# Linear attention into a two-layer MLP: the first microseconds of a kernel listed anew

## Chip, cores and metric

The kernel runs on one core of one Trainium2 chip. The metric is device time in microseconds, the median of several runs. Beside the runs there is one profiled execution, of which the trace tells every instruction; its span is a little shorter than its time. TensorE is PE, VectorE DVE, ScalarE ACT, GpSimd POOL and SyncE SP in what follows.

## The reference

Two parts follow on each other. The first is a linear attention with a decaying state, for 4 batches, 8 heads, 768 tokens and 48 values a head:

```python
for t in range(S):
    cur = np.einsum('bhd,bhe->bhde', u[None] * kt, vt)
    y[:, :, t] = np.einsum('bhd,bhde->bhe', rt, state + cur)
    state = w[None, :, :, None] * state + np.einsum('bhd,bhe->bhde', kt, vt)
```

The second takes y as 3072 rows of 384 through two matrices, with a leaky ReLU between them:

```python
h = x @ w_in                    # 384 to 2048
g = np.maximum(0.01 * h, h)
return (g @ w_out).astype(np.float32)   # 2048 to 384
```

## The kernel before

**Stages.** The tokens are cut in chunks of 128, and one chunk of one batch, with all 8 heads, is a stage: 24 stages n, batch n % 4, chunk n // 4. Inside a chunk the attention is written as matmuls. r and k are first multiplied with tables of powers of w (qtab, ktab, line 344), which are made once: w is spread over 128 partitions by a matmul with a vector of ones (line 295), ACT takes the logarithm (line 301), and an exponential with a scale that depends on the token gives the table (line 306). One state per batch is carried from chunk to chunk, so stage n needs the state that stage n - 4 left.

**Steps of a stage**, by the letters that the list of the work uses:

- k, r, v: the loads of the stage (line 222, by POOL's queue; those of stage 0 by ACT's and SP's, line 213). wi and wo are the quarters of the two matrices (lines 232 and 236), also on POOL's queue.
- P: product of r (q) or k with its table, on DVE (line 344). T: its transpose by a matmul with the identity, on PE (line 398). t: the copy of that out of PSUM, on ACT (line 412) or, with @, on DVE (line 410). From stage 8 on, X with a T is a transposing DMA on SP's queue instead (line 349).
- A: scores of the 8 heads, on PE (line 423). M: their causal mask, on DVE, in two halves (line 432, from stage 8 on line 436).
- X: product of the transposed q and k (line 359, DVE); D: its sum with w and u over each head (line 451, PE); Q: v scaled by that (line 366, DVE). From stage 8 on q (lines 373 to 377, DVE) and Q (line 384, POOL) take their place.
- K: the stage's addition to the state (line 464, PE). S: the new state (lines 522 to 527, DVE).
- Y: the stage's output (lines 550 and 557, PE); y: its copy into xT (line 571, ACT).
- G n.g: a quarter of the first matrix for one stage, 12 matmuls of 128 columns (line 596); g: the leaky ReLU (line 606, ACT). J m.j: an eighth for two stages, 6 matmuls of 256 columns (line 619); j: line 629. H: the second matrix for a stage (line 643, PE); h: the copy and the store on SP's queue (lines 655 and 657).
- F n: n matmuls of ones that nobody reads (line 260), here called fillings.

**Order.** For the first four stages' MLP, and for the attention of the stages ahead of it, everything stands in one list, `ORDER`, written out by hand. Each name adds instructions to its engine, and each engine runs its own in the order of the list. The waits follow from what is read and written (`Sched.add`, `Sched.resolve`): a step behind a waiting one on the same engine waits too. PSUM has eight banks, which `take` and `give` pass around in the order of the list. After the list comes a regular loop over pairs of stages, from stage 6 on for the MLP (lines 696 to 727).

**Single steps** of the list, once each: w, u (rows), w8, u8 (by heads) are small loads; tcol, exps the exponents; ones, one, v0z, qk0, wlz memsets on DVE; id, tri the identity and the triangle on POOL; table the loading of ACT's functions; id8 a small float32 identity and wu8 the product of w and u (DVE); Cm columns of w and w times u by heads (lines 484 and 485, PE), Wl their logarithm, C their copies, W the decay table of the state (lines 497, 504 and 512); u16, U, utab the spread of u (lines 317, 321 and 326).

Before the change w is spread in two halves of 192 columns, each with a matmul, a logarithm and two exponentials of its own: bcA, bcB, lnA, lnB, ktabA, qtabA, ktabB, qtabB.

Of the kernel before, what the change touches and what calls it, by code (L numbers as in the profile page):

```python
# [17 lines left out]
HD = H * D  # L18
# [6 lines left out]
FIRST, NB, PACE = 6, B, 3  # L25
TURNED, DIAG, CARRY, EXACT = 8, 8, 4, 1
ORDER = """
w k0 r0 u8 w8 u ones tcol wi0 v0z r2 table exps one id wlz qk0 F6 bcA r1 id8 F2 bcB lnA k1 u16 wu8 ktabA F1 Cm k2 lnB U
qtabA ktabB v0 utab P0k qtabB Wl wi3 F6 T0k P0q W C tri t0k@ F1 T0q v1 P1q t0q P2q F6 T1q X0 r3 A0 P1k t1q T2q M0a T1k
k3 t2q D0 P2k F1 K0 t1k Q0 T2k v2 M0b t2k F1 A1 X1 v5 F2 Y0 X2 M1b A2 k4 y0 D2 M1a D1 K1 G0.0 k5 Q1 M2b G0.3 g0.0 wi1  # L30
P3q Y1 P3k g0.3 r4 S1 T3q y1 K2 Q2 T3k t3q v3 G1.3 S2 t3k M2a G1.0 r5 g1.3 P4k Y2 X3 g1.0 r8 P5k A3 S0 y2 K5 M3b r6 T5k
G2.3 t5k S5 k7 G2.0 g2.3 M3a G1.1 k9 g2.0 P4q G0.1 g1.1 wi2 T4k g0.1 D3 P5q K3 r7 T4q Q3 t4k T5q G2.1 S3 t5q k6 P8q Y3
t4q P6q X5 A5 v4 g2.1 P7k A4 X4 y3 D5 T6q M4a wo3 T7k t6q G3.0 M5a v8 t7k G3.3 Q5 g3.0 wo0 M5b D4 G3.1 g3.3 P9k k8 G2.2
M4b g3.1 P7q G1.2 wo2 g2.2 P6k T7q v6 g1.2 T6k t7q@ K4 Y5 t6k Q4 wo1 A7 y5 X6 A6 k11 S4 Y4 M7b v9 D6 y4 G3.2 M6a v10
J2.4 M6b g3.2 J2.3 M7a v11 j2.4 J2.5 X7 j2.3 r10 D7 J2.1 j2.5 q8 r9 J2.2 j2.1 J2.6 r11 j2.2 P8k J2.0 j2.6 v7 X8T K8 Q6
K6 j2.0 G0.2 k10 S6 Y6 g0.2 S8 J2.7 y6 H1 j2.7 P11k K9 H2 h1 S9 P10q H0 h2 P9q q9 X9T P11q K7 Q9 H3 Q7 h0 X11T S7 P10k
X10T Q8 Y7 h3 A9 y7 A8 M9a M8a M9b M8b k12 r12 v12 k13 r13 v13
"""


# [4 lines left out]
class Sched:  # L45
# [7 lines left out]

    def add(self, eng, emit, R=(), W=(), dma=None):
        o = Op()
        o.eng, o.emit, o.dma, o.inc, o.val = eng, emit, dma, False, None
        deps = []
        for key in R:
            w = self.writer.get(key)
            if w is not None:  # L60
                deps.append((w, True))
        for key in W:
            w = self.writer.get(key)
            if w is not None:
                deps.append((w, False))
            for r in self.readers.get(key, ()):
                deps.append((r, False))
        o.deps = []
        for d, raw in deps:
            if d.dma is None and d.eng == eng and dma is None and (eng == "pe" or not raw):  # L70
                continue
            if d is not o and d not in o.deps:
                o.deps.append(d)
        for key in R:
            self.readers.setdefault(key, []).append(o)
        for key in W:
            self.writer[key] = o
            self.readers[key] = []
        self.ops.append(o)
        return o  # L80
# [47 lines left out]
def bass_rwkv5_eagle__then__act_leaky_relu_kernel(  # L128
# [19 lines left out]
    r_sb = SB("r_sb", [128, NST, HD])  # L148
    k_sb = SB("k_sb", [128, NST, HD])
    v_sb = SB("v_sb", [128, NST, H * E])  # L150
    w_row = SB("w_row", [1, HD], FP32)
    u_row = SB("u_row", [1, HD], FP32)
    one_row = SB("one_row", [1, 128], FP32)
    u_row16 = SB("u_row16", [1, HD])
    w_head = SB("w_head", [H, D], FP32)
    u_head = SB("u_head", [H, D], FP32)
# [4 lines left out]
    lnw = SB("lnw", [128, HD], FP32)  # L161
# [3 lines left out]
    qtab = SB("qtab", [128, HD])  # L165
    ktab = SB("ktab", [128, HD])
    tcol = SB("tcol", [128, 1], FP32)
    qexp = SB("qexp", [128, 1], FP32)
    kexp = SB("kexp", [128, 1], FP32)
    wcol = SB("wcol", [128, NP], FP32)  # L170
    wl = SB("wl", [128, NP, 2 * D])
    ones = SB("ones", [128, 256])
    mask = SB("mask", [128, 128])
    ident = SB("ident", [128, 128])
    ku = [SB(f"ku{i}", [128, HD]) for i in range(4)]
# [2 lines left out]
    qk = [SB(f"qk{i}", [128, 2 * H, E]) for i in range(NQK)]  # L178
# [5 lines left out]
    xT = [SB(f"xT{i}", [128, NSL, 256]) for i in range(NX)]  # L184
    gT = [SB(f"gT{i}", [128, NFB, 256]) for i in range(NG)]
    out_sb = [SB(f"out_sb{i}", [128, HD], FP32) for i in range(NO)]
    ps = [ctx.enter_context(nc.psum_tensor(f"ps{i}", [128, 512], FP32)) for i in range(8)]

    V, A, PE, SP, G = nc.vector, nc.scalar, nc.tensor, nc.sync, nc.gpsimd
    sch = Sched(ctx, nc)  # L190
    add = sch.add
    free = list(range(8))

    def take():
        i = free.pop(0)
# [19 lines left out]
    def load_one(n, which, pace=()):  # L215
# [39 lines left out]
    def fill(n):  # L255
        i = free[0]

        def emit():
            for _ in range(n):
                last = PE.matmul(ps[i][:, 0:256], ones[:, 0:128], ones[:, 0:256], start=True, stop=True)  # L260
            return last

        add("pe", emit, R=["ones"], W=[("ps", i), f"fill{n}"])

    def identity():
        add("pool", lambda: G.affine_select(ident[:, :], ones[:, 0:128], pattern=[[1, 128]], compare_op=ALU.is_equal,
                                            fill=0.0, base=0, channel_multiplier=-1), R=["ones"], W=["ident"])

# [18 lines left out]
        add("dve", lambda: V.memset(wl[:, :, :], 0.0), W=["wl"])  # L287
        add("dve", lambda: V.memset(wu[:, :, :], 0.0), W=["wu"])

    half_bank = {}  # L290

    def spread_w(half):
        ps_w, key = half_bank[half] = take()
        cols = slice(192 * half, 192 * half + 192)
        add("pe", lambda: PE.matmul(ps_w[:, cols], one_row[:, :], w_row[:, cols], start=True, stop=True),  # L295
            R=["one_row", "w_row"], W=[key])

    def log_w(half):
        ps_w, key = half_bank[half]
        cols = slice(192 * half, 192 * half + 192)  # L300
        add("act", lambda: A.activation(lnw[:, cols], ps_w[:, cols], AF.Ln), R=[key], W=[("lnw", half)])
        give(key)

    def table(dst, exps, name, half):
        cols = slice(192 * half, 192 * half + 192)
        add("act", lambda: A.activation(dst[:, cols], lnw[:, cols], AF.Exp, scale=exps[:, 0:1]),
            R=[("lnw", half), name + "exp"], W=[(name + "tab", half)])

    def small_identity():
        add("dve", lambda: V.tensor_copy(ident8[:, :], ident[0:H, 0:H]), R=["ident"], W=["ident8"])  # L310
# [21 lines left out]
    def hd(x):  # L332
        return x.rearrange("p (h d) -> p h d", d=D)

    def k_of(n):
        return k_sb[:, n, :] if n >= EXACT else k_f[:, n, :]

    def r_of(n):
        return r_sb[:, n, :] if n >= EXACT else r_f[:, n, :]

    def prep_half(n, half):
        iq = n % NQK
        src, tab, name, done = ((r_of(n), qtab, "r", "qp"), (k_of(n), ktab, "k", "kp"))[half]
        add("dve", lambda: V.tensor_tensor(qk[iq][:, H * half:H * half + H, 0:D], hd(src), hd(tab[:, :]), ALU.mult),  # L344
            R=[(name, n), ("qk"[half] + "tab", 0), ("qk"[half] + "tab", 1), ("qk0", iq)], W=[(done, iq)])

    def turn_dma(n):
        iq = n % NQK
# [3 lines left out]
    def prep(n):  # L352
        prep_half(n, 0)
        prep_half(n, 1)
        turn_dma(n)
# [293 lines left out]
    def g2_out(n, c0=0, c1=HD):  # L649
# [9 lines left out]

    half_of = {"q": 0, "k": 1, "a": 0, "b": 1}  # L660
    single = {
        "w": lambda: add("sp", lambda: SP.dma_start(w_row[:, :], row(w)), W=["w_row"], dma="w"),
        "w8": lambda: add("sp", lambda: SP.dma_start(w_head[:, :], by_head(w)), W=["w_head"], dma="w8"),
        "u8": lambda: add("act", lambda: A.dma_start(u_head[:, :], by_head(u)), W=["u_head"], dma="u8"),
        "u": lambda: add("act", lambda: A.dma_start(u_row[:, :], row(u)), W=["u_row"], dma="u"),
        "one": lambda: add("dve", lambda: V.memset(one_row[:, :], 1.0), W=["one_row"]),
        "tcol": tokens, "ones": filled, "exps": exponents, "v0z": zero_v, "qk0": zero_qk, "wlz": zero_w,
        "id": identity, "tri": triangle, "table": preload, "id8": small_identity, "wu8": wu_product,
        "bcA": lambda: spread_w(0), "bcB": lambda: spread_w(1), "lnA": lambda: log_w(0), "lnB": lambda: log_w(1),
        "qtabA": lambda: table(qtab, qexp, "q", 0), "qtabB": lambda: table(qtab, qexp, "q", 1),  # L670
        "ktabA": lambda: table(ktab, kexp, "k", 0), "ktabB": lambda: table(ktab, kexp, "k", 1),
        "Cm": columns_mm, "Wl": log_columns, "C": decay_columns, "W": decay_table,
        "u16": u_cast, "U": u_spread, "utab": u_table,
    }
# [110 lines left out]
```

## Time and profile before

| | |
|---|---|
| median of 3 runs | 170.57 us (170.1 to 171.39) |
| the profiled execution: its own time | 170.54 us |
| its span | 168.8 us |
| PE busy | 164.0 us, 97% of the span |
| DVE busy | 107.6 us, 64% |
| POOL busy | 103.8 us, 61% |
| ACT busy | 92.5 us, 55% |
| chain that ended last, on PE | 96% |
| of it, line 260 (fillings) | 2.5% |
| POOL's loads | k 5.1, r 5.6, v 6.0, wi 5.6, wo 7.9 us from issue to landing (medians) |

Start times below are counted from the start of the span. The profile's rows in forty slices tell the busy share of each engine in tenths, 9 for 90% and more. The chain of work that ended last is followed back from the last instruction: at each step to what released it, or to the instruction before it on its engine. Lines of the timeline give the start, the length, the engine, the line, what is written from what, the shapes, and in brackets the idle time before and what ended it.

### The profile page before, as it was taken

Reading aid. Unit: us, or ns where it says so; the run is one execution under the profiler, and the core shown is the slowest. Engines: PE = TensorE matmul, PEld = TensorE weight load, DVE = VectorE, ACT = ScalarE, POOL = GpSimd, SP = SyncE. Lnnn points to the kernel's source line nnn. Section 1 sums busy time; section 2 is a strip of 40 time slices with the busy share of each in tenths; the row PEclk is TensorE's granted clock in tenths of the full one; section 3 lists DMA queues with packets and bytes.
Section 4 is the critical chain, followed back from the end, with each engine's and each line's share of the span. In section 5 each row is a group of like instructions: output and inputs, shape, how many; then the busy total and the mean of one; then the engine's idle time right before and its main releaser. Section 6 shows DMA issues by size and latency. Waiting matters only on the chain.

```text
span 168.8 us, 4933 instructions
## 1 busy us (share of the span) xinstructions
PE 164.0 (97%) x2127; PEld 124.4 (74%) x2127; DVE 107.6 (64%) x215; ACT 92.5 (55%) x172; POOL 103.8 (61%) x117
## 2 busy tenths in 40 slices
PE   5999999899999999999999999999999999999994
PEld 3577899798667867867867867768768668668663
DVE  7379989884376999999859959969866050000000
ACT  3855899587123933933834835735637538449221
POOL 7999999990059979897993993993707200000000
PEclk9999999999999999999999999999999999999999
DMA  6999999999999999969999299299941011011022
GB/s 106 155 170 133 163 163 173 185 190 149 110 177 144 161 62 153 193 82 169 126 140 171 55 143 177 65 109 131 147 122 50 0 50 47 0 50 47 25 74 93
DMA packets 99146, 19.67 MB, mean 117 GB/s; under 512 B 92338, under 2 KB 99124, under 8 KB 99124
## 3 DMA queue, kind: packets, MB, share of 16 engines
q0 software_dynamic: 76512, 10.03, 93.1%
q1 hardware_dynamic: 21554, 9.12, 25.2%
q8 instruction: 17, 0.28, 0.6%
q10 hardware_dynamic: 1058, 0.20, 0.6%
q14 instruction: 5, 0.04, 0.1%
HBM read 20.45 MB, written 4.72 MB: 149 GB/s over the span
## 4 chain that ended last, share of the span: by engine, by line
PE 96%; DVE 1%; issue 1%; ACT 0%; DVEq 0%
PE ps L643 37%; PE ps L619 31%; PE ps L596 6%; PE ps L557 6%; PE ps L423 4%; PE ps L260 2%; PE ps L464 2%; PE ps L398 2%; PE ps L295 1%; PE ps L550 1%; DVE v_sb L280 1%; PE ps L451 1%; PE ps L321 0%; DVE qk L344 0%; ACT out_sb L655 0%
## 5 line engine op out<-in xcount | busy, mean ns | idle before, releaser
L643 PE MATMUL ps<-w_out_sb,gT 128*128 128x384 bf16 (+2 forms) x400 | 65.7, 320 | 0.0
L619 PE MATMUL ps<-xT,w_in_sb 128*128 128x256 bf16 x480 | 54.3, 273 | 0.0
L643 PEld LDWEIGHTS ps<-w_out_sb,gT 128*128 128x128 bf16 x400 | 37.9, 98 | 22.1
L619 PEld LDWEIGHTS ps<-xT,w_in_sb 128*128 128x128 bf16 x480 | 46.7, 98 | 6.5 <-ACT xT L571 0.2
L384 POOL TENSOR_TENSOR at<-ident,s_tok 128x512 bf16<-128x512 bf16 x32 | 35.0, 1121 | 26.8 <-DVE s_tok L377 26.8
L629 ACT ACTIVATE gT<-ps 128x512 bf16<-128x512 f32 x80 | 47.8, 597 | 6.2 <-PE ps L619 1.3
L655 ACT ACTIVATE out_sb<-ps 128x384 f32<-128x384 f32 (+2 forms) x25 | 11.9, 477 | 52.9 <-PE ps L643 52.9
L436 DVE CAST_PREDICATED at<-mask,ps 128x512 bf16<-128x512 uint16 x32 | 19.9, 684 | 15.5 <-PE ps L423 15.5
L222 POOL DMA_DIRECT2D v_sb<-in_v_dram x24 | 22.5, 953 | 0.0
L222 POOL DMA_DIRECT2D k_sb<-in_k_dram x23 | 21.6, 947 | 0.0
L222 POOL DMA_DIRECT2D r_sb<-in_r_dram x23 | 21.1, 943 | 0.0
L571 ACT ACTIVATE xT<-ps 128x384 bf16<-128x384 f32 x24 | 11.0, 492 | 6.5 <-PE ps L557 6.5
L344 DVE TENSOR_TENSOR qk<-r_sb,qtab 128x384 bf16<-128x384 bf16 x23 | 13.4, 592 | 1.9 <-DMA r_sb<-in_r_dram 1.9
L344 DVE TENSOR_TENSOR qk<-k_sb,ktab 128x384 bf16<-128x384 bf16 x23 | 13.9, 606 | 0.0
L375 DVE TENSOR_TENSOR rku<-r_sb,ku 128x384 bf16<-128x384 bf16 x16 | 12.7, 794 | 0.5
L525 DVE TENSOR_TENSOR sum_t<-ps,st 128x384 bf16<-128x384 f32 x16 | 8.8, 550 | 5.2 <-PE ps L464 5.2
L596 PE MATMUL ps<-xT,w_in_sb 128*128 128x128 bf16 x192 | 12.0, 219 | 0.0
L557 PE MATMUL ps<-at,v_sb 128*32 128x128 bf16 x384 | 11.1, 219 | 0.6 <-issue 0.6
L432 DVE TENSOR_TENSOR at<-ps,mask 128x512 bf16<-128x512 f32 x16 | 10.5, 682 | 0.9 <-PE ps L423 0.9
L606 ACT ACTIVATE gT<-ps 128x512 bf16<-128x512 f32 x16 | 9.6, 600 | 2.7 <-PE ps L596 2.1
L596 PEld LDWEIGHTS ps<-xT,w_in_sb 128*128 128x128 bf16 x192 | 10.9, 98 | 0.1
L557 PEld LDWEIGHTS ps<-at,v_sb 128*32 128x32 bf16 x384 | 8.7, 97 | 1.1 <-issue 0.7
(60 smaller groups left out, 131.7 us busy)
## 6 DMA issues: line engine op xcount, KB each, us to landing
out_dram<-out_sb SPq DMA_DIRECT2D x23, 192.0 KB, 3.9
v_sb<-in_v_dram POOLq DMA_DIRECT2D x24, 96.0 KB, 6.0
r_sb<-in_r_dram POOLq DMA_DIRECT2D x23, 96.0 KB, 5.6
k_sb<-in_k_dram POOLq DMA_DIRECT2D x23, 96.0 KB, 5.1
w_in_sb<-in_moe_w_in_dram POOLq DMA_DIRECT2D x4, 384.0 KB, 5.6
w_out_sb<-in_moe_w_out_dram POOLq DMA_DIRECT2D x4, 384.0 KB, 7.9
tp<-qk SPq DMA_TRANSPOSE x16, 4.6
k_f<-in_k_dram ACTq DMA_DIRECT2D x1, 192.0 KB, 2.8
```

Source lines behind the costliest of these rows:

```text
L222: add("pool", lambda: G.dma_start(dst, src), R=pace, W=[(which, n)], dma=f"{which}{n}")
L344: add("dve", lambda: V.tensor_tensor(qk[iq][:, H * half:H * half + H, 0:D], hd(src), hd(tab[:, :]), ALU.mult), R=[(name, n), ("qk"[half] + ...
L375: add("dve", lambda: V.tensor_tensor(rku[i2][:, :], r_of(n), ku[i2][:, :], ALU.mult), R=[("r", n), ("ku", i2)], W=[("rku", i2)])
L384: add("pool", lambda hh=hh, s_of=s_of: G.tensor_tensor(at[ia][:, hh, :, :], ident[:, :].unsqueeze(1).to_broadcast([128, NP, 128]), s_of.un ...
L436: add("dve", lambda: V.copy_predicated(at[n % NAT][:, hh, :, :], mask[:, :].bitcast(mybir.dt.uint16).unsqueeze(1).to_broadcast([128, NP, 1 ...
L557: last = PE.matmul(ps_y[32 * q:32 * q + 32, 128 * s:128 * s + 128], a, m, start=not whole and step == 0, stop=step == len(columns[q]) - 1)
L571: add("act", lambda: A.activation(xT[m % NX][:, :, 128 * half:128 * half + 128], ps_y[:, 0:HD].rearrange("p (s t) -> p s t", t=128), AF.Copy),
L596: last = PE.matmul(ps_g[:, 128 * f:128 * f + 128], w_in_sb[:, s, 128 * fb:128 * fb + 128], xT[ix][:, s, t], start=s == 0, stop=s == NSL - 1)
L619: last = PE.matmul(ps_g[:, 256 * f:256 * f + 256], w_in_sb[:, s, 128 * fb:128 * fb + 128], xT[ix][:, s, :], start=s == 0, stop=s == NSL - 1)
L629: add("act", lambda: A.activation(gT[ig][:, 2 * j:2 * j + 2, :].rearrange("p f t -> p (f t)"), ps_g[:, :], AF.Prelu, alpha=0.01), R=[key], ...
L643: last = PE.matmul(ps_o[:, 0:c1 - c0], gT[ig][:, s, 128 * half:128 * half + 128], w_out_sb[:, s, c0:c1], start=s == 0, stop=s == NFB - 1)
L655: add("act", lambda: A.activation(out_sb[io][:, c0:c1], ps_o[:, 0:c1 - c0], AF.Copy), R=[key], W=held)
```

## The change

- w is loaded into two partitions, 0 and 64, 192 values each, instead of one with 384; the vector of ones that spreads it has 128 partitions instead of one. One step, bc, holds the two matmuls, into two PSUM banks that follow on each other.
- One logarithm reads both banks and writes 384 columns (lnw). Each table is one exponential of 384 columns (qtab, ktab), q first.
- The small loads u8 and u are issued by SP instead of ACT, and w8 stands with them.
- A filling is a matmul of 128 columns instead of 256, and the tile of ones has 128 columns.
- The list is written anew: another order of the stages (stage 5 early, stage 2 late), of the loads and of the parts of the matrices, other fillings (F12 and F13 around bc, thirty between T5q and Y0, sixteen more up to J2.7), the copies t1q, t1k and t6q on DVE and t0k on ACT. The useful steps are otherwise the same ones, and the regular loop is unchanged.

```diff
 ORDER = """
-w k0 r0 u8 w8 u ones tcol wi0 v0z r2 table exps one id wlz qk0 F6 bcA r1 id8 F2 bcB lnA k1 u16 wu8 ktabA F1 Cm k2 lnB U
-qtabA ktabB v0 utab P0k qtabB Wl wi3 F6 T0k P0q W C tri t0k@ F1 T0q v1 P1q t0q P2q F6 T1q X0 r3 A0 P1k t1q T2q M0a T1k
...
+w k0 r0 w8 u8 u wlz tcol k1 ones table one exps qk0 r1 v0z r5 F12 bc wi2 lnw id qtab wu8 v0 id8 u16 F13 Cm P0q ktab U
+k3 P1q T0q Wl P0k utab T1q r3 P1k t0q T0k C P5q W T1k t1q@ k4 T5q t0k t1k@ tri t5q F2 A0 X0 v1 X1 F2 A1 M0a F3 D0 wi1
+M0b F5 D1 F1 K0 k5 P3k P3q F11 T3k Q0 r4 F3 T3q P4k t3k F3 Y0 M1b v3 t3q T4k M1a y0 F2 K1 A3 r2 t4k Q1 F1 G0.2 M3a wi3
+F1 Y1 S1 g0.2 G0.1 M3b v5 y1 X3 F2 G1.2 r7 P5k g0.1 S0 T5k g1.2 D3 P4q k6 G1.1 Q3 t5k T4q r6 g1.1 K3 P2q Y3 S3 t4q T2q
+k2 X5 y3 F2 A5 X4 F1 A4 t2q M5a G3.2 v4 M4b F1 G3.3 wi0 g3.2 M4a D4 D5 G0.3 g3.3 k7 M5b G1.3 P7q g0.3 v7 Q5 K5 P6k G3.1
+g1.3 S5 wo2 T6k g3.1 Y5 P6q v2 P2k t6k T6q Q4 y5 r10 F2 K4 T2k t6q@ T7q t2k Y4 v6 t7q@ A6 y4 S4 F1 A2 wo3 G1.0 M6a r11
+F1 J2.7 P7k g1.0 M6b wo0 J2.0 j2.7 M2b J2.6 v8 j2.0 X2 M2a J2.2 j2.6 wo1 K7 J2.1 j2.2 v9 S7 K2 J2.4 j2.1 S2 r9 G0.0
+P10q j2.4 r8 K6 J2.3 g0.0 S6 v11 D2 G3.0 j2.3 X6 Q2 k8 T7k g3.0 D6 J2.5 Q6 t7k k11 Y2 P11q j2.5 X7 A7 k9 y2 Y6 M7a k10
+D7 M7b y6 G2.1 Q7 v10 G2.0 g2.1 G2.3 g2.0 G2.2 g2.3 H1 g2.2 P9q P8q H2 h1 P8k q8 X8T K8 H0 h2 P9k Q8 S8 X9T P10k P11k
+K9 X10T H3 h0 q9 X11T S9 Q9 Y7 h3 A9 y7 A8 M8a M9a M9b M8b k12 r12 v12 k13 r13 v13
 """
@@
-    w_row = SB("w_row", [1, HD], FP32)
+    w_row = SB("w_row", [128, HD // 2], FP32)
-    one_row = SB("one_row", [1, 128], FP32)
+    one_row = SB("one_row", [128, 128], FP32)
-    ones = SB("ones", [128, 256])
+    ones = SB("ones", [128, 128])
@@
-    ps = [ctx.enter_context(nc.psum_tensor(f"ps{i}", [128, 512], FP32)) for i in range(8)]
+    ps_all = ctx.enter_context(nc.psum_tensor("ps", [128, 8, 512], FP32))
+    ps = [ps_all[:, i, :] for i in range(8)]
@@
-                last = PE.matmul(ps[i][:, 0:256], ones[:, 0:128], ones[:, 0:256], start=True, stop=True)
+                last = PE.matmul(ps[i][:, 0:128], ones[:, :], ones[:, :], start=True, stop=True)
@@
+    def spread_w():
+        for half in range(2):
+            w_bank.append(take())
...
+        def emit():
+            for half in range(2):
+                at0 = slice(64 * half, 64 * half + 1)
+                last = PE.matmul(w_bank[half][0][:, 0:192], one_row[at0, :], w_row[at0, :], start=True, stop=True)
+            return last
...
+    def log_w():
+        i = w_bank[0][1][1]
+        add("act", lambda: A.activation(lnw[:, :].rearrange("p (two c) -> p two c", two=2),
+                                        ps_all[:, i:i + 2, 0:192], AF.Ln),
+            R=[w_bank[0][1], w_bank[1][1]], W=["lnw"])
...
+    def table(dst, exps, name):
+        add("act", lambda: A.activation(dst[:, :], lnw[:, :], AF.Exp, scale=exps[:, 0:1]),
+            R=["lnw", name + "exp"], W=[name + "tab"])
@@
-        "w": lambda: add("sp", lambda: SP.dma_start(w_row[:, :], row(w)), W=["w_row"], dma="w"),
+        "w": lambda: add("sp", lambda: SP.dma_start(
+            w_row[0:65:64, :], dram(w, 0, [[HD // 2, 2], [1, HD // 2]])),
+            W=["w_row"], dma="w"),
-        "u8": lambda: add("act", lambda: A.dma_start(u_head[:, :], by_head(u)), W=["u_head"], dma="u8"),
-        "u": lambda: add("act", lambda: A.dma_start(u_row[:, :], row(u)), W=["u_row"], dma="u"),
+        "u8": lambda: add("sp", lambda: SP.dma_start(u_head[:, :], by_head(u)), W=["u_head"], dma="u8"),
+        "u": lambda: add("sp", lambda: SP.dma_start(u_row[:, :], row(u)), W=["u_row"], dma="u"),
```

More of the change, by code (lines that the diff above doesn't have):

```diff
@@ L27 @@
 ORDER = """
-w k0 r0 u8 w8 u ones tcol wi0 v0z r2 table exps one id wlz qk0 F6 bcA r1 id8 F2 bcB lnA k1 u16 wu8 ktabA F1 Cm k2 lnB U
-qtabA ktabB v0 utab P0k qtabB Wl wi3 F6 T0k P0q W C tri t0k@ F1 T0q v1 P1q t0q P2q F6 T1q X0 r3 A0 P1k t1q T2q M0a T1k
[L30 to L37, printed above, removed]
+w k0 r0 w8 u8 u wlz tcol k1 ones table one exps qk0 r1 v0z r5 F12 bc wi2 lnw id qtab wu8 v0 id8 u16 F13 Cm P0q ktab U
[8 more added lines that the diff above has]
+K9 X10T H3 h0 q9 X11T S9 Q9 Y7 h3 A9 y7 A8 M8a M9a M9b M8b k12 r12 v12 k13 r13 v13
 """
@@ L288, in zero_w @@
         add("dve", lambda: V.memset(wu[:, :, :], 0.0), W=["wu"])
[L290 to L307, printed above, removed]
+    w_bank = []
+    def spread_w():
+        for half in range(2):
+            w_bank.append(take())
+        assert w_bank[1][1][1] == w_bank[0][1][1] + 1
+        def emit():
[3 more added lines that the diff above has]
+            return last
+        add("pe", emit, R=["one_row", "w_row"], W=[w_bank[0][1], w_bank[1][1]])
+    def log_w():
[3 more added lines that the diff above has]
+            R=[w_bank[0][1], w_bank[1][1]], W=["lnw"])
+        give(w_bank[0][1])
+        give(w_bank[1][1])
+    def table(dst, exps, name):
+        add("act", lambda: A.activation(dst[:, :], lnw[:, :], AF.Exp, scale=exps[:, 0:1]),
+            R=["lnw", name + "exp"], W=[name + "tab"])
     def small_identity():
@@ L344, in prep_half @@
         add("dve", lambda: V.tensor_tensor(qk[iq][:, H * half:H * half + H, 0:D], hd(src), hd(tab[:, :]), ALU.mult),
-            R=[(name, n), ("qk"[half] + "tab", 0), ("qk"[half] + "tab", 1), ("qk0", iq)], W=[(done, iq)])
+            R=[(name, n), "qk"[half] + "tab", ("qk0", iq)], W=[(done, iq)])
     def turn_dma(n):
@@ L668, in bass_rwkv5_eagle__then__act_leaky_relu_kernel @@
         "id": identity, "tri": triangle, "table": preload, "id8": small_identity, "wu8": wu_product,
-        "bcA": lambda: spread_w(0), "bcB": lambda: spread_w(1), "lnA": lambda: log_w(0), "lnB": lambda: log_w(1),
-        "qtabA": lambda: table(qtab, qexp, "q", 0), "qtabB": lambda: table(qtab, qexp, "q", 1),
-        "ktabA": lambda: table(ktab, kexp, "k", 0), "ktabB": lambda: table(ktab, kexp, "k", 1),
+        "bc": spread_w, "lnw": log_w, "qtab": lambda: table(qtab, qexp, "q"), "ktab": lambda: table(ktab, kexp, "k"),
         "Cm": columns_mm, "Wl": log_columns, "C": decay_columns, "W": decay_table,
```

## The prediction

> **What bounds the kernel now.** I read the page's busy row by slices first, then the chain of work that ended last, then the timeline of the first 14 us, and the landings last. All times are us from the start of the span.
>
> ```profile
> PE   5999999899999999999999999999999999999994
> ...
> DVE  7379989884376999999859959969866050000000
> ...
> PEclk9999999999999999999999999999999999999999
> DMA  6999999999999999969999299299941011011022
> ```
>
> A slice is 4.22 us. PE is busy from the second slice to the end, and so are the DMA engines up to the fifteenth (63 us). DVE is nearly full in slices 4 to 7 (13 to 30).
>
> ```profile
> 9.24 1.28 PE ps L260 x6
> 10.52 0.43 PE ps L398 x4
> 10.94 0.56 PE ps L423 x8
> ...
> 13.01 0.11 PE ps L260
> ...
> 20.43 0.22 PE ps L398 x4
> ...
> 31.39 0.56 issue
> ```
>
> This is the chain (start, us, engine and line). From 13.77 on it is PE without a break, save 0.56 at 31.39 in which PE waits for nothing that the profile shows; from 53.52 on it is the regular loop, which the change doesn't touch. So only idle time, filling (L260) and slow work of PE ahead of 53.52 can be won. The chain also shows the speed: four transposes (L398) take 0.43 at 10.52 and 0.22 at 20.43, a filling 0.21 at 9.24 and 0.11 at 13.01. PE works at half speed until somewhere between 10.94 and 13.01. The granted clock stands at 9 from the first slice, so that row does not tell of it; the durations do.
>
> ```profile
> 3.15 0.97 PE L295 MATMUL ps<-w_row,one_row 1*128 1x192 f32 x2 [0.43 <-DVE one_row L666]
> ...
> 4.16 0.33 ACT L301 ACTIVATE lnw<-ps 128x192 f32<-128x192 f32 x1 [0.59 <-PE ps L295]
> ...
> 6.74 0.56 DVE L344 TENSOR_TENSOR qk<-k_f,ktab 128x384 bf16<-128x384 f32 x1 [1.94 <-ACT ktab L306]
> ...
> 11.60 0.69 DVE L432 TENSOR_TENSOR at<-ps,mask 128x512 bf16<-128x512 f32 x1 [0.93 <-PE ps L423]
> ```
>
> The timeline (start, length, in brackets the idle time before) has the way to the first useful work: spread w, logarithm, tables, first product at 6.74, first scores masked at 11.60. The first output tile Y0 follows at 13.77.
>
> **The change, part by part.**
>
> *w, logarithm, tables.* DVE now begins with the zeroing of wl and wu (0.22 + 0.06), then half of the old ones (0.27 for 256 columns), so the first filling starts at about 1.4 (1.25 before) and twelve of 128 columns, half of 0.21 each, end at 2.7. The vector one_row, which held the spread until 3.15, is then there by 1.6. The spread (two halves in one step) costs between 0.97, if the halves run side by side, and 0.97 + 0.94 = 1.91, one after the other. Nearest is the L423 row, whose matmuls also lie in two halves of the rows: 0.07 each against 0.107 for whole ones; between the ends by that ratio, 1.3: done at 4.0. The logarithm over 384 columns is priced at 0.33 + 0.16 = 0.49, since 384 and 512 columns take 0.49 and 0.60 in L571 and L412; a table at 0.44 + 0.16 = 0.60. With 0.2 of waiting between them, qtab stands at 5.4. Were the spread serial, at 6.0.
>
> *What holds it then.* On POOL four loads instead of two precede the identity; at 0.9 each it moves from 3.26 to 5.0, done at 5.3. On DVE the small identity (0.39) waits for it, and the first product P0q is queued right behind: P0q at 5.65, not 6.74. P1q, P0k (ktab at 6.3), P1k, C and P5q follow to 7.8 (0.56 for float32, 0.35 for bf16).
>
> *Small loads.* u8 and u leave ACT (0.73 + 0.23 of issuing) for SP behind w, r0 and w8. The table load, 1.28, starts at 1.3 instead of 2.29; worth nothing, as the logarithm waits for PE. u now lands between 4.7 and 6.0 (issued at 2.9, plus less than 1.8, or plus the 3.1 of r_f ahead of it). Its cast is ahead of ktab on ACT: nothing at the early end, 0.6 of ktab at the late one. I take the early end, since in the trace the cast ran at 4.52 behind the same large loads. Nothing else is on SP until the first transposing DMA.
>
> *First transposes.* PE: 13 fillings end at 5.4, under the wait for the small identity; were that gone they would cost 0.2. Then the columns, u, and T0q from 6.6; five T at half speed, 0.43 each, to 8.8. ACT sets A0: utab, t0q, W (0.74), t0k, at 0.5 to 0.6, end at 9.0. A0 at 9.1 (10.87 before), first mask 9.9 (11.60 before), and the DVE list from there (0.60 a mask, 0.27 a product, 0.46 a scaled v, starts apart) lets Y0 go at 12.25.
>
> *Fillings up to Y0.* Thirty stand between T5q and Y0, with A0, A1, D0, D1, K0, T3k, T3q. Added in PE's order with half speed until 11.4, as before, Y0 comes at 13.1; at full speed from A0 on, DVE sets 12.25. Dense work (fillings, transposes) began at 6.71 before and full speed came 4.2 to 6.3 later. After the change it begins at 6.6, with 1.4 of fillings ahead of a gap, so I take the same or up to 1 us sooner, and for Y0 12.7: 1.1 earlier. By then one T and one D more are done (0.22 + 0.08): 1.4 in all.
>
> [...]
>
> *Fillings and waits after Y0.* Sixteen fillings of 128 columns follow between Y0 and J2.7, at 0.055 each (half of 0.11): 0.9 if PE would not have waited there, nothing if it would. With Y0 at 12.7, PE reaches G0.2, Y1 and T5k within 0.3 of when ACT and DVE let them go, so I take 0.8. DVE gets two evictions more (t1q, t1k and t6q in place of t0k), 0.69 each; ACT's work covers less, but PE has the G groups, 0.67 each, that wait for neither, and in the trace DVE is idle 0.67 at 23 and 0.53 at 30. I price them at nothing; uncovered, 1.2 at most (two starts of 0.6).
>
> *Loads in a new order.* At equal counts of large and small loads ahead, I give each load the landing of its counterpart. They come 0.2 to 1.5 ahead of their user: r2 at 18.1 (as the k issued at 13.6, 4.6 later) for P2q, v4 24.7 for Q4, v2 30.4 for K2, v6 31.9 for K6, wo1 at 39.1 (29.5 + 9.6) for H1, which stood at 41.51. Nothing, with up to 1 us if one slips. The 0.56 at 31.39 I leave in place, as nothing shows its cause.
>
> *Sum.* 1.4 - 0.8 = 0.6 gained, kept to the end. The profiled execution took 170.54 (span 168.8), the median of the runs is 170.57: no correction. 170.54 - 0.6 = 169.9.
>
> **The rivals.**
>
> *Everything early (0.15).* Full speed from A0, Y0 at 12.25, the later fillings inside waits, and the 0.56 gone: 1.5 + 0.3 + 0.56 - 0.4 = 2.0, 168.5. For it: DVE alone allows it. Against: it needs three things together, and wo1 allows H1 only 2.4 earlier.
>
> *Full speed later (0.12), the one on the other side.* Between 8.8 and 11.6 the new list has PE waiting for t0k, and two-column matmuls (D0, D1) between fillings; F11 at 11.6 is the first dense run after. If the 4.7 us from 6.71 to about 11.4 are counted from there, full speed comes at 16.3; 4.9 us of work at half speed lose 2.4, and with Y0 at 13.1 the sum starts from 0.1 gained: 172.8. It decides from 15.0 on (1.8 lost). Against: the fillings were dense enough with such pauses before 10.94. [...]
>
> *Transposing DMAs late (0.15).* X8T stood at 37.05 and landed 8.3 later, X9T at 47.83 and 2.7 later. Now r8 and k8 are loaded last, and X9T is queued on SP behind the output of H2, which ends at 46.1; with the copy of 0.49, X9T goes at 46.6 and lands at 49.3 to 54.9. A9 wants it at 52.3: nothing to 2.6 lost, 172.5 at worst, most likely 171.
>
> *It doesn't do what it says (0.10).* Half speed until 11.4 or later and PE bound from T0q: the fillings take back all, 170.5.
>
> **How the numbers follow.** My forecast, the likeliest, has 0.48 and its own range 169.2 to 170.5: 169.9. The range to hold 8 in 10 runs from 168.5 (all early) to 172.3, which leaves out the full delay of the clock and the end of the late transposes. About 1%, 1.7 us, is what a measurement of this kernel can tell from no change: below 168.9 is faster, above 172.3 slower. Faster: the early case, 0.15, and a little for errors of the sum: 0.17. Slower: the late clock, the worst third of the transposes and a load that slips beside them, 0.19. Within: 0.64.
>
> **What would show it.** In the timeline after: P0q near 5.65 behind the small identity (right), or later behind the table (spread serial, or u late); A0 near 9.1 behind t0k; a transpose of 0.22 first seen before or after 11.4 tells which clock case holds; Y0 near 12.7. In the chain, L260 pieces after Y0 and no idle pieces; the start of H1 near 40.9 and of the regular loop near 52.9, both with the whole gain in them. An idle piece ahead of A9 shows the late transposes. Wrong altogether if PE waits between 14 and 40 for loads or DVE by more than 1 us, since each such wait goes to the end undiminished.

## The result and the profile after

The kernel after takes 171.42 us (median of 22 runs, 170.38 to 172.72), the kernel before, on the same chips, 170.06 (22 runs, 169.28 to 171.39): ratio 1.0089, interval 1.0063 to 1.0115. It is 1.4 us slower, where 0.6 faster was forecast; the time is inside the range and, by the bound of 1%, no change, but it went the other way. The 22 times lie in two groups: fifteen from 170.38 to 171.61 and seven from 172.20 to 172.72. The profiled execution took 170.38 (span 168.6) and is the fastest of all, so it shows where a good execution loses, not where the median does.

The page's busy row by slices, kernel after:

```profile
PE   6899999999999999999999999999999999999994
```

PE has a little more in the first slice (6 for 5) and a little less in the second (8 for 9); nothing in this row looks like a loss. The chain of work that ended last does:

```profile
9.07 0.78 POOL v_sb L223
9.86 6.43 DMA w_in_sb<-in_moe_w_in_dram
16.29 0.05 issue
16.34 0.84 PE ps L605 x12
...
53.36 5.41 PE ps L628 x48
```

Before, the chain was on PE from 3.15 on, save 1.1 ahead of 12.61 that belong to DVE and the 0.56 at 31.39. Now it runs along POOL's queue, load behind load, to the tenth load, wi1; PE gets it at 16.34 (G0.1) and is the chain only from there. The first H begins at 41.35 instead of 41.51 and the regular loop at 53.36 instead of 53.52: the profiled execution gains 0.16, as its times do (170.54 to 170.38).

The timeline of the first 14.8 us (the lines that answer to those shown of before, and PE's scores):

```profile
3.12 1.01 PE L301 MATMUL ps<-w_row,one_row 1*128 1x192 f32 x4 [0.32 <-DMA w_row<-in_w_dram]
4.18 0.49 ACT L308 ACTIVATE lnw<-ps 128x384 f32<-128x384 f32 x1 [1.65 <-PE ps L301]
5.51 0.20 DVE L322 TENSOR_TENSOR wu_head<-w_head,u_head 8x48 f32<-8x48 f32 x1 [1.57 <-DMA u_head<-in_u_dram]
5.71 0.54 DVE L353 TENSOR_TENSOR qk<-r_f,qtab 128x384 bf16<-128x384 f32 x1
6.65 0.36 DVE L353 TENSOR_TENSOR qk<-r_sb,qtab 128x384 bf16<-128x384 bf16 x1 [0.40 <-DMA r_sb<-in_r_dram]
9.58 0.61 PE L432 MATMUL ps<-tp 48*128 48x128 bf16 x8
10.31 1.28 DVE L441 TENSOR_TENSOR at<-ps,mask 128x512 bf16<-128x512 f32 x2
10.37 0.40 PE L432 MATMUL ps<-tp 48*128 48x128 bf16 x8
12.98 0.33 PE L559 MATMUL ps<-ident,vs 128*128 128x128 bf16 x3
```

The first product comes at 5.71 (6.74 before), the first mask at 10.31 (11.60), Y0 at 12.98 (L550 at 13.68 before, in the same view). Eight scores take 0.61 at 9.58 and 0.40 at 10.37: full speed came between the two, earlier than before. But two waits for loads are new here, and the waits of the first 54 us (us in all, times, longest) hold more:

```profile
DVE qk L353 <- DMA r_sb<-in_r_dram: 3.3, 5, 2.0
DVE wu_head L322 <- DMA u_head<-in_u_dram: 1.6, 1, 1.6
DVE qk L353 <- DMA k_sb<-in_k_dram: 1.3, 2, 1.1
PE ps L605 <- DMA w_in_sb<-in_moe_w_in_dram: 0.4, 1, 0.4
```

DVE waited 1.1 for r's before, and the view of before has no line for k's. The longest of them, 2.0 for r and 1.1 for k, stand at 41.48 and 43.65, where PE goes on without a pause; between 7 and 20 such a wait is 0.2 to 0.4, and those for r, k and v come to 1.6. Loads are wanted sooner, and in this profile they also take longer. DMA issues (count, size, median us from issue to landing), first of before, then of after:

```profile
v_sb<-in_v_dram POOLq DMA_DIRECT2D x24, 96.0 KB, 6.0
r_sb<-in_r_dram POOLq DMA_DIRECT2D x23, 96.0 KB, 5.6
k_sb<-in_k_dram POOLq DMA_DIRECT2D x23, 96.0 KB, 5.1
w_in_sb<-in_moe_w_in_dram POOLq DMA_DIRECT2D x4, 384.0 KB, 5.6
w_out_sb<-in_moe_w_out_dram POOLq DMA_DIRECT2D x4, 384.0 KB, 7.9
```

```profile
v_sb<-in_v_dram POOLq DMA_DIRECT2D x24, 96.0 KB, 6.3
k_sb<-in_k_dram POOLq DMA_DIRECT2D x23, 96.0 KB, 6.1
r_sb<-in_r_dram POOLq DMA_DIRECT2D x23, 96.0 KB, 5.9
w_in_sb<-in_moe_w_in_dram POOLq DMA_DIRECT2D x4, 384.0 KB, 6.8
w_out_sb<-in_moe_w_out_dram POOLq DMA_DIRECT2D x4, 384.0 KB, 9.3
```

POOL issues its loads at the same pace (15 by 15 us before and 16 after, 21 by 20 us in both), yet by these medians k's, w_in's and w_out's land 1.0 to 1.4 us later and r's and v's 0.3. What lengthens them is not shown, and it is not the new order alone: e1 below keeps the old order of these loads, and its page has 5.9, 6.8 and 9.2 for k, w_in and w_out.

### The profile page after: what moved, and what is told of

The parts are those of the page before. It is cut to its first block, busy times and chain, and to the rows that moved or that the text cites. A ratio compares the mean times of both kernels' runs of the same rounds, so it can differ in the third digit from the quotient of the medians.

```text
span 168.6 us, 5011 instructions
## 1 busy us (share of the span) xinstructions
PE 163.7 (97%) x2170; PEld 126.1 (75%) x2170; DVE 106.9 (63%) x217; ACT 90.8 (54%) x167; POOL 103.6 (61%) x117
## 4 chain that ended last, share of the span: by engine, by line
PE 89%; POOL 5%; DMA 4%; issue 0%; ACT 0%; POOLq 0%
PE ps L652 37%; PE ps L628 31%; PE ps L605 6%; PE ps L566 6%; DMA w_in_sb<-in_moe_w_in_dram 4%; PE ps L432 4%; PE ps L473 2%; POOL k_sb L223 2%; POOL r_sb L223 2%; PE ps L407 1%; POOL v_sb L223 1%; PE ps L559 1%; PE ps L261 0%; POOL w_in_sb L233 0%; PE ps L460 0%
## 5 line engine op out<-in xcount | busy, mean ns | idle before, releaser
L353 DVE TENSOR_TENSOR qk<-r_sb,qtab 128x384 bf16<-128x384 bf16 x23 | 14.2, 617 | 3.8 <-DMA r_sb<-in_r_dram 3.8
L353 DVE TENSOR_TENSOR qk<-k_sb,ktab 128x384 bf16<-128x384 bf16 x23 | 13.0, 570 | 1.3 <-DMA k_sb<-in_k_dram 1.3
L605 PE MATMUL ps<-xT,w_in_sb 128*128 128x128 bf16 x192 | 12.5, 219 | 0.4 <-DMA w_in_sb<-in_moe_w_in_dram 0.4
L384 DVE TENSOR_TENSOR rku<-r_sb,ku 128x384 bf16<-128x384 bf16 x16 | 10.8, 675 | 0.6
L261 PE MATMUL ps<-ones 128*128 128x128 bf16 x69 | 8.5, 257 | 1.3 <-DVE ones L251 1.3
```

What stands on the lines that cost most here:

```text
L384: add("dve", lambda: V.tensor_tensor(rku[i2][:, :], r_of(n), ku[i2][:, :], ALU.mult), R=[("r", n), ("ku", i2)], W=[("rku", i2)])
L605: last = PE.matmul(ps_g[:, 128 * f:128 * f + 128], w_in_sb[:, s, 128 * fb:128 * fb + 128], xT[ix][:, s, t], start=s == 0, stop=s == NSL - 1)
```

## The experiments

Four theories were held, as they formed. **A**: the new list wants loads of POOL's queue (r's, v1, wi1) before they land, and such a wait goes to the end undiminished. **B**: full speed of PE comes late in some executions of the new list, by the pauses that the list leaves PE ahead of it. **C**: the other parts of the front (one logarithm over two banks, longer exponentials) cost time by themselves. **D**: r0 and the small loads behind it on SP's queue land late. Runs beside the kernel before on the same chip; the ratio is to that.

**Front or list.** e1 has the old list with the new functions (halves joined, fillings doubled in number at half the width, small loads on SP). e2 has the new list with the old front.

```
e1: -w k0 r0 u8 w8 u ones ... F6 bcA r1 id8 F2 bcB lnA ... lnB U qtabA ktabB ... qtabB
    +w k0 r0 w8 u8 u ones ... F12 bc r1 id8 F4 lnw ... U qtab
e2: -bc ... lnw ... qtab ... ktab          (of the new list)
    +bcA bcB ... lnA lnB ... qtabA qtabB ... ktabA ktabB
```

> The old list with the new front alone: one spread, one logarithm, two tables of 384 columns, small loads on SyncE's queue, every filling of 256 columns replaced by two of 128. Theory A (the new list asks for its loads too early: in the changed kernel G0.1 waits for a quarter of w_in that landed at 16.28, and VectorE waits 5.0 us for loads of r, k and v between 7 and 20): the loss is in the list, so this kernel is at the time before or up to 0.5 us under it. Theory B (full speed of TensorE comes at a different moment in each execution, and the new list stands it worse): also at the time before, since the fillings and the old order are kept. Theory C (the new front itself loses): 1 us or more above the time before.

> The new list with the old front: two spreads, two logarithms, four table halves, u and u8 issued by ScalarE; fillings of 128 columns as in the new list. Theories A and B: as slow as the changed kernel or up to 0.7 us slower, 1.3 to 2.1 us above before. Theory C: at the time before or under it.

e1 took 172.16 (ratio 1.013, 1.0105 to 1.0156), e2 171.46 (1.0079, 1.005 to 1.0108). The list alone costs what the change costs; but the front alone, on the old list, costs still more, against A's claim that it is harmless. The 5.0 us of waits that A named for 7 to 20 are those of the first 54 us (3.3 for r, 1.3 for k and 0.4 for v). Chain of e1:

```profile
1.99 0.46 SPq L674
...
2.50 5.29 DMA u_head<-in_u_dram
...
7.82 0.34 DVE wu_head L322
```

u8, 1.5 KB, was issued at 2.50 and landed at 7.80; DVE stood at wu8 for it, with the products queued behind. This is D. Chain of e2, whose u8 goes by ACT:

```profile
6.99 5.10 DMA r_sb<-in_r_dram
12.09 0.03 issue
12.11 0.37 DVE qk L345
```

There the list's own load r3 (5.10 from issue to landing) holds DVE until 12.09: A.

**The front taken apart** (D against C, on the old list). e7 is e1 with w in one partition, two matmuls over its halves; e8 is e1 with the small loads ahead of r0.

```
e7: -w_row[0:65:64, :], dram(w, 0, [[HD // 2, 2], [1, HD // 2]])
    +w_row[:, :], row(w)
e8: -w k0 r0 w8 u8 u
    +w k0 w8 u8 u r0
```

> The front alone on the old list, but w in one partition as before, spread by two matmuls one behind the other in one step. The load of w then takes 0.33 of issuing and not 0.66, so r0 is issued at 1.2 and not 1.5. Theory D, if those 0.3 are what makes r0 late: 170.2 to 171.0, against 172.16 for the front alone. Theory D, if the small loads' place behind r0 is enough: 171.5 to 172.2. Theory C (something else in the front, such as the one logarithm or the longer exponentials): 172.

> The front alone on the old list, with w8, u8 and u issued ahead of r0 on SyncE's queue. Theory D: u8 lands before 4.5, the small loads hold nothing, r0 is wanted only at 7.2 to 7.7; the median is 169.6 to 170.4, against 172.16 for the front alone. Theory C: 172.

e7: 170.32 (0.9987, 0.9965 to 1.0009). e8: 169.94 (0.9975, 0.9951 to 0.9999). Either edit wins back all that e1 lost. Both keep the one logarithm and the longer exponentials, so C falls. Why e7 helps is in the issuing on SP's queue (start, length), e1 first, then e7:

```profile
0.80 0.66 SPq L671 DMA_DIRECT2D w_row<-in_w_dram  x1
1.52 0.42 SPq L214 DMA_DIRECT2D r_f<-in_r_dram  x1
```

```profile
0.80 0.33 SPq L671 DMA_DIRECT2D w_row<-in_w_dram  x1
1.19 0.42 SPq L214 DMA_DIRECT2D r_f<-in_r_dram  x1
```

The load to two partitions took twice the issuing, so r0 goes 0.33 later, in among the first loads of POOL's queue. From issue to landing r0 took 6.0 in e1 and 3.6 in e7, against 3.1 in before and 3.8 in after. That the edit wins back the loss is shown by the runs. That it does so by these 0.33 is read from one profile of each and not shown: after issues r0 at the same 1.52 and has it 2.2 sooner than e1, and e7 also spreads both halves from one partition (ACT's logarithm waits 2.1 for PE there, 1.7 in e1).

**D on the new list.** e5 puts r0 first, on ACT's queue, and k0 last on SP's.

```
-{"k": ("act", A), "r": ("sp", SP)}      -w k0 r0 w8 u8 u
+{"k": ("sp", SP), "r": ("act", A)}      +w r0 w8 u8 u k0
```

> The changed kernel with r0 issued by ScalarE as its first load and, on SyncE's queue, w, w8, u8 and u ahead of k0. Theory D (r0 and the small loads queued behind it land late and at another time in each execution: r0 at 4.3 before, 5.3 after, 7.5 in the front alone, u8 behind it at 3.9, 5.5 and 7.8; the new list needs wu8, the small identity and P0q from 5.5 on, the old one only from 6.5 to 7.7): u8 lands before 4.5, P0q waits for the small identity alone, and the median falls to 169.0 to 170.0, with the runs above 171.5 gone unless k0 now lands after 6.5. Theory B (the moment of full speed): 171.4 with the same spread. Theory A (loads by GpSimd's queue): 171.2 to 171.6.

172.48 (1.0084, 1.0055 to 1.0112), above what any of the theories had. The small loads came in time (wu8 at 3.86, P0q at 5.66, where after has 5.51 and 5.71) and nothing was gained: in its chain DVE waits for a load of POOL's queue, r1, whose product is the next one ("2.47 4.44 DMA r_sb<-in_r_dram"), and full speed came at about 13.4. So on the new list D is not what binds.

**Fillings and order before full speed** (B). e3 has more fillings ahead of the first transposes, e4 none after F13, e6 makes the k products first and the small columns last.

```
e3: -F12 ... F13 ... U k3           e4: -F2 F2 F3 F5 F1 F11 ... F1   (all behind F13)
    +F15 ... F18 ... U F3 k3
e6: -qtab wu8 v0 id8 u16 F13 Cm P0q ktab U k3 P1q T0q ... T0k
    +ktab v0 F13 P0k qtab k3 P1k T0k T1k P0q ... T0q T1q wu8 id8 Cm U
```

> The changed kernel with more filling ahead of the first transposes: 15 and 18 in place of 12 and 13, and 3 more behind the spread of u, so that TensorE has nearly no gap from 1.3 on. Theory B: full speed comes earlier than in the changed kernel in most executions, the median falls by 0.7 us or more and the slow half of its runs (171.5 to 172.7) is gone. Theory A: within 0.2 us of the changed kernel with the same spread between runs, since no load moves.

> The changed kernel without the 46 fillings behind the first two groups. Theory B: full speed comes 1 to 3 us later, the median rises by 1 us or more. Theory A: the fillings stood in waits for loads or cost up to 0.9 us, so the time stays or falls by up to 0.9 us.

> The changed kernel with the k table and the products of k ahead of those of r, and the steps that need u8 and w8 (wu8, the small identity, the columns, the spread of u) behind the first products and transposes; the loads are left as they are. Theory D: r0 is wanted 0.9 and u8 1.5 us later than in the changed kernel, the work that waits for neither comes first, and the median falls by 0.6 to 1.5 us, to 170.0 to 170.8. Theories A and B: 171.2 to 171.7.

e3: 170.95 (1.0053, 1.0022 to 1.0085), eight runs from 170.17 to 171.09 and four from 172.54 to 173.02. e4: 170.95 (1.0048, 1.0022 to 1.0074). e6: 172.89 (1.0142, 1.0114 to 1.017), above what any theory had. Fillings are not what the loss is: without them (44 fewer; the list has fourteen behind Y0, not the sixteen reckoned so far) 0.5% remains. That went against what B expected of it. The intervals of e3 and e4 overlap that of after (1.0063 to 1.0115), so that they are better than after is not shown either.

**Full speed moved in time** (B). In e9 to e12 all loads wait until ten tiles have been zeroed by DVE, so that everything begins 9.6 (new list: e9, e10) or 9.7 us (old list: e11, e12) later; e9 and e11 fill PE meanwhile. This adds work and changes no output.

```
+def gate(): for t in gT + xT + out_sb: memset(t, 0.0), W=["gate"]     # all loads: +R=["gate"]
e10: +ones gate w k0 r0 ...    e9: +ones F100 gate w k0 r0 ... -F13 +F36
e12: +ones gate w k0 r0 ...    e11: +ones F50 gate w k0 r0 ...
```

> The changed kernel with everything but one memset and 100 fillings put off: all loads wait until VectorE has zeroed ten tiles (some 8 us), while TensorE fills from 1.3 on, and 36 instead of 13 fillings stand behind the spread of w. TensorE is thus at full speed before the first useful work, and the loads stand to the work as in the changed kernel. All of it is longer by the delay T, which the trace tells as the start of the load of w less 0.8. Theory B (the moment of full speed is what the new list stands worse): less T, the time is 169.0 to 170.2, the runs lie within 1 us, and it is faster than the old list under the same treatment. Theories A and D (loads): less T, 170.6 to 171.2, a spread of 2 us as in the changed kernel, and slower than the old list under the same treatment by 0.8 to 1.3.

> The same delay of the changed kernel without the fillings in it: TensorE starts cold. Both theories: less T, the time and spread of the changed kernel, 171.4 with 170.4 to 172.7. Theory B: 1 to 2.5 us over the one with the fillings; A and D: 0.3 to 0.8 over it, for the five transposes at half speed.

> The kernel before with the same delay and 50 fillings of 256 columns in it. Theory B: less T, 169.2 to 169.8 and over the new list so treated. A and D: the same time, but 0.8 to 1.3 under the new list so treated.

> The kernel before with the delay and no fillings in it. All theories: less T, the time before, 170.0 to 170.6.

Less the delay: e9 171.3, e10 172.7, e11 170.65, e12 171.0. The new list is thus 0.7 behind the old one with the fillings and 1.7 without. The filling did not keep full speed, so the design failed. The busy time of e9 by stretches (the stretch and its length, then PE, PEld, DVE, ACT and POOL with the number of instructions in brackets, the granted clock, the share and GB/s of the DMA):

```profile
8.00:12.00 4.00, 1.39 (x25) 1.21 (x22) 3.58 (x18) 1.18 (x1) 1.34 (x2) 0.98 0.12 25
12.00:16.00 4.00, 3.15 (x25) 2.72 (x26) 1.41 (x3) 1.21 (x3) 4.00 (x6) 0.50 1.86 157
16.00:20.00 4.00, 4.00 (x40) 3.45 (x39) 2.75 (x10) 2.62 (x7) 4.00 (x7) 0.50 1.88 160
20.00:24.00 4.00, 3.98 (x64) 3.22 (x62) 3.84 (x9) 1.52 (x4) 4.00 (x5) 0.74 1.99 169
```

The fillings end at 9.39, and 2.45 us into the pause full speed was taken away, at 11.84 (a mean clock of 0.98 over these 4 us); it came back at 22.08 (0.74). The durations agree: two fillings take 0.42 at 20.70, five 0.44 at 22.63. That is 10.24 us. In it PE was busy 79% of the stretch from 12 and all of the one from 16, and the clock stayed at 0.50 in both: here busy by this table did not bring full speed back. Matmuls of one row (L302, 1.01 from 12.85; L331, 0.49 from 18.17) and of eight (0.34 and 0.32 from 17.74) count as busy in it too; whether that is why is not shown. Still, e9 and e10 differ in nothing but fillings: of e10's six runs four lie at 182.23 to 182.89 and two at 180.16 and 180.54, all six of e9's at 180.62 to 181.62. No upper group was seen with the fillings there; six runs of each are few.

**The kernel after, profiled twice more** (no edit), and two lists mended by all that was known. e13: r0 and k0 on ACT, the small loads alone on SP, the small columns behind the first transposes, u's spread put behind D7, r5 put back. e14: the same front on the old list.

```
e13: -w k0 r0 w8 u8 u wlz ... r5 F12 ... Cm P0q ktab U ... C P5q W T1k
     +w r0 w8 u8 u k0 wlz ... F15 ... F19 P0q ktab ... C X1 M0a ... r2 r5 ... D7 U M7b
e14: -w k0 r0 u8 w8 u ones ... u16 wu8 ... Cm k2 lnB U
     +w k0 w8 u8 u r0 ones ... id8 wu8 F4 lnw k1 Cm ... g1.2 u16 ... K4 U
```

> The changed kernel again, for a second profile. [...] Theory D (loads): the time follows the landing of u8 and r0 (5.5 and 5.3 in the first), 1 us for 1 us, and full speed has no say.

> The changed kernel once more, for a third profile: as for the second.

> The new list mended on both counts: r0 and k0 on ScalarE's queue, w, w8, u8 and u alone on SyncE's; the spread of u, which nothing needs before stage 8, put behind G2.1; stage 5's early product and transpose put back; more filling ahead of the first transposes, and the columns behind them, so that TensorE's dense work runs from 4.3 to A0. Theory B: no run in the slow group (none over 171.0), median 168.6 to 169.6. Theory D alone: the median falls by 0.7 to 1.2 against the changed kernel, to 170.2 to 170.7, and a group 1.7 us over the rest stays.

> The old list with the new front and the loads mended (r0 and k0 on ScalarE's queue, the small ones alone on SyncE's), the spread of u put behind Y5, fewer fillings ahead of the first transpose, which comes at about 6.2 instead of 8.0. Theory D: 168.8 to 169.8, under the kernel before. [...]

e13: 171.48 (1.0072, 1.0048 to 1.0096): its chain runs through wu8, which I had put behind the copies and which ran at 9.81 only. e14: 170.58 (1.0034, 1.0014 to 1.0054), with r0 landing only at 7.21. Neither beat before. after_p2 took 170.84, after_p3 171.28. Their chains:

```profile
8.99 5.78 DMA v_sb<-in_v_dram
14.77 0.04 issue
```

```profile
9.86 7.39 DMA w_in_sb<-in_moe_w_in_dram
17.24 0.05 issue
```

The same kernel waits for v1 in after_p2 and for wi1 in after_p3. In the first profile and in after_p3 wi1 was issued at 9.86; it landed at 16.29 and 17.24, 0.95 apart, and the times are 0.90 apart. By the durations of fillings and scores, full speed came just before 10 in after_p2 and between 11.3 and 11.8 in after_p3. So the time of after_p2 does not follow it (0.46 above the first profile's, with full speed no later), and that of after_p3 is set by wi1, on its chain from 9.86 to 17.24.

**One load moved, either way** (A against B). e15 takes r5 and its product, transposes and copy out of the front, so that loads up to wi1 go a place sooner; with it stage 4's scores move ahead of stage 5's. e16 issues wi1 behind k5 and r4.

```
e15: -v0z r5 F12 ... T0k C P5q W ... k4 T5q t0k ... tri t5q F2 ... r2 t4k
     +v0z F12    ... T0k C W     ... k4 t0k     ... tri F2     ... r2 r5 t4k
e16: -D0 wi1 M0b F5 D1 F1 K0 k5 P3k P3q F11 T3k Q0 r4 F3
     +D0 M0b F5 D1 F1 K0 k5 P3k P3q F11 T3k Q0 r4 wi1 F3
```

> One load (r5) and its product, transposes and copy go back behind r2, so that every load from v0 to wi1 is issued one place sooner on POOL's queue; nothing else is changed from the kernel after. If the new list loses because loads of POOL's queue are wanted too early, wi1 lands about 0.75 us sooner (near 15.5) and the median is 0.5 to 0.8 below that of the kernel after (171.4), near 170.7. If only the moment of full speed of TensorE decides, or late small loads on SyncE's queue do, there is no gain: 171.2 to 171.8.

> The load wi1 is issued behind k5 and r4 instead of ahead of them; nothing else is changed from the kernel after. If a late load goes to the end one for one, wi1 lands 1.5 to 2 us later (near 18), G0.1 waits for it, and the median is 1.0 to 1.4 above that of the kernel after: 172.4 to 172.8, less what k5 and r4 win by going sooner. If only the moment of full speed of TensorE decides, or late small loads on SyncE's queue do: 171.4 as after.

e15: 172.30 (1.0094, 1.0057 to 1.0131), three runs from 171.58 to 171.92 and three from 172.68 to 172.83. e16: 172.18 (1.0089, 1.0054 to 1.0123), 171.51 to 172.60 without a gap. A's gain for e15 did not come. For e16 the profile is as A says (172.04; "11.59 6.41 DMA w_in_sb<-in_moe_w_in_dram", landed 18.00): landing and time of three executions are 16.29 and 170.38, 17.24 and 171.28, 18.00 and 172.04, always 154.0 to 154.1 apart. And its fastest run is 1.1 above that of after (before's fastest, on that chip, 0.3 above). But the ratio of the median did not move, which suggests that in many runs of after something else sets the end. e15's profiled execution (172.68) is the first one of an upper group that was seen, and its chain shows what:

```profile
9.07 0.60 ACT tp L421
...
9.73 0.61 PE ps L432 x8
10.34 0.33 PE ps L261 x2
10.66 0.54 PE ps L432 x5
...
12.81 1.17 PE ps L261 x11
13.98 0.43 PE ps L407 x4
14.41 0.32 PE ps L261 x3
14.73 0.43 PE ps L407 x4
15.16 0.18 PE ps L261 x3
15.34 0.17 PE ps L559 x3
```

Four transposes (L407) still take 0.43 at 14.73, three fillings 0.18 at 15.16: full speed came at 15.1, not between 9.6 and 10.4. No load is in this chain after 6; PE works at half speed until Y0, which starts at 15.34. The same stretch of e3 (the fillings are L262 there, the transposes L408), at full speed:

```profile
12.31 0.61 PE ps L262 x11
12.92 0.22 PE ps L408 x4
```

In e6 the eleven fillings took 1.17 at 13.62 and four transposes 0.29 at 15.54. By such durations full speed came at about 11 in e3 (profiled at 170.46), 13.4 in e5 (171.22), 15.1 in e15 (172.68) and 15.6 in e6 (172.80). Some of the traces also hold a record of the clock that was granted, and where it has the moment the two agree: 10.23 in after, 9.98 in after_p2, 13.33 in e5, 15.07 in e15, 15.55 in e6, and 11.49 in before. PE's work from the first score to Y0 is the same in e3, e5, e6, e15 and after; by the timeline it took 3.40 us in after (9.58 to 12.98), 3.49 in e3 (10.05 to 13.54), 4.71 in e5 (9.56 to 14.27), 5.45 in e15 (9.73 to 15.18) and 5.30 in e6 (10.54 to 15.84). Full speed 4.1 us later made it 1.96 longer from e3 to e15: half, as it must where half of the speed is missing. From that start of Y0 to the time it is 156.9 in e3, 157.0 in e5 and e6 and 157.5 in e15, so a late Y0 goes to the end undiminished. No profile of after itself shows full speed that late.

## Why the prediction was wrong, point by point

**w, logarithm, tables: right.** The spread took 1.01 (the halves run side by side, the lower end of 0.97 to 1.91; 1.3 was taken), the logarithm 0.49 and a table 0.61 as priced. qtab stood at 5.38 (5.4). Part of that is luck: the sum lets the spread begin at 2.7 and has no wait for w itself, which landed only just before 3.12, and the shorter spread made up for most of it.

**What holds it then: right in place, partly in cause.** P0q at 5.71 (5.65), P0q behind id8 on DVE. But id8 was there late because of wu8 ahead of it, which waited 1.57 for u8. In e5, with u8 early, P0q stood at 5.66, so the wait cost 0.05 there.

**Small loads: failed.** "I take the early end" priced them at nothing. In the profiled execution u8 landed at 5.5 and the columns began at 6.18, so it cost little; with the same front on the old list u8 landed at 7.80 and the change lost 1.3% (e1). The step missed that u8 (not u) is the one DVE waits for, and that r0, ahead in the queue, can itself land late (7.5 in e1); that w's longer issue is what puts r0 off is likely by e7, not shown. e5 shows that on the new list its removal gains nothing by itself.

**First transposes and fillings up to Y0: right in the profiled execution, too sure of the clock.** First scores at 9.58 (9.1), first mask 10.31 (9.9), Y0 at 12.98, 0.7 earlier (1.1): what Y0 lacks was lost by the first scores. Full speed came 1.3 us sooner, 10.23 for 11.49 ("the same or up to 1 us sooner"). The three profiles of after have it at 10.23, at 9.98 and past 11.3. The prediction treated this as one moment for the kernel. Its rival, full speed later (172.8, chance 0.12, at 16.3), is what e15 (172.68, at 15.1) and e6 (172.80, at 15.6) show in kind and size; why it came late in them is not shown. Seven of 22 runs of after lie at 172.2 to 172.7, near e15's and e6's height, though before took 170.66 and 170.64 beside those two and 170.06 beside after. That those seven had the late clock is argued from this, since none of them was profiled. The rival of late transposing DMAs was not seen: the chain goes through A9 (52.76) without a gap.

**Fillings after Y0: right.** There are fourteen of them, not sixteen. Ten on the chain after 16.34 take 0.77, and four between Y0 and there 0.22: 1.0 (0.8).

**Loads in a new order: failed, and this set the profiled execution.** "I give each load the landing of its counterpart" and "nothing". The counterparts' landings (w_in 5.6, k 5.1) became 6.8 and 6.1 in this profile. wi1, which the sum did not even list, was issued at 9.86; at 5.6 it would have landed at 15.5 and at 6.43 it came at 16.29, while PE was ready at 15.99. Its price is 0.35 of idle PE in the best execution, and it started G0.1 another 0.95 later in after_p3. The prediction's own sign of being wrong, a wait of PE for a load between 14 and 40, is there in all three profiles of after.

**The sum.** For the profiled execution, gains of 0.7 (Y0), some 0.3 (work done ahead) and 0.56 (the unexplained "issue" is not there any more), less 1.0 of fillings and 0.35 for wi1: 0.2, measured 0.16. The forecast of 0.6 was thus 0.4 off there, and that it was no further off is luck, since it had left the 0.56 in place. The other 1.0 to the median is put down to executions in which a load lands later or full speed comes later, and the prediction reckoned a single execution as if it were the median. Of before, the profiled execution lies 0.48 above its median of 22 runs, of after 1.04 below: as much of the miss is there as in any term.

**What stays open.** How the loss of 1.4 divides. The median of the fifteen lower runs is 171.16, 1.1 above before, and loads account for such times where they were seen (170.84, 171.28); the upper seven raise the rest. But e15, with its loads sooner, was no better even in its lower runs (171.58 to 171.92, some 1.2 above before on that chip), which weren't profiled. I take it that several waits of nearly the same height, r3, v1, wi1, u8 and full speed, stand behind one another in the new list; taking one away (e3, e5, e13, e15) uncovers the next. Each of them is seen on the chain of some kernel here, full speed as slow work of PE; their shares of the loss are not shown.

## What to carry to other kernels

When a prologue is pulled forward, the loads behind it have to come forward as well, and a landing is not a fixed number (the median of the w_in loads was 6.8, 6.5 and 7.6 in three profiles of after): price every load from its new issue with the slowest landing of its kind, not with its counterpart's, and look first at the load nearest to its user. A profiled execution shows one draw of the landings and of the clock (the first of after took 170.38, the median is 171.42), so price the spread and not the one sample. The small gain that was to be had here lay elsewhere: the new front with the small loads ahead of the large one on their queue (e8), 0.25% with an interval that all but reaches 1.

## What was not expected of the hardware

- A load to two partitions took 0.66 us of SP's issuing, to one 0.33. Behind it on that queue r0 took from 3.8 (after) to 6.0 us (e1) to land, and a load of 1.5 KB behind r0 in e1 5.29.
- wi1, issued at the same moment of the same kernel (9.86), took 6.43 and 7.39 us.
- Full speed of PE came between 10 and 15.6 us after the start in kernels whose PE work from the first score on is the same, and PE was busy through 4 us (16 to 20 in e9) at a granted clock of 0.50, with part of that work matmuls of one row and of eight.
- In e9 full speed was lost 2.45 us after the last filling, and the record of the clock has it granted at 5.02 (28 fillings took 2.88 us up to 4, 66 the 4.00 us from there to 8), lost at 11.84 and granted again at 22.08: 6.83 and 10.24 us apart.
